# A new order for all steps of a fused linear-attention and gated feed-forward kernel, with other engines and buffers for some of them

## The chip, the core and the metric

The kernel runs on one core of a Trainium2 chip. The metric is the device time of one execution in microseconds (us), inputs and output in HBM. The times and the profiled execution below are of this kernel on such a core.

## The reference, cut to what matters

```python
def _attn_ref(q, k, v, f_logit):          # (4, 8, 768, 48) each, float32
    f = 1.0 / (1.0 + np.exp(-f_logit))
    for t in range(S):                    # S = 768
        state = f[:, :, t, :, None] * state + np.einsum('bhd,bhe->bhde', k[:, :, t], v[:, :, t])
        y[:, :, t] = np.einsum('bhd,bhde->bhe', q[:, :, t], state)

def _moe_ref(x, w_in, w_out):             # x (3072, 384), w_in (384, 2048), w_out (2048, 384)
    h = x @ w_in
    g = h * np.cos(h)
    return g @ w_out

x = y.transpose(0, 2, 1, 3).reshape(3072, 384)
```

The first part is a gated linear attention over 4 batches, 8 heads and 768 positions; its output, with the heads put side by side, is the input of the second part, two matrix products with a gate between them.

## The kernel before, in words

**Pairs and units.** The attention is done in chunks of 128 positions, two chunks at a time: a *pair* is 256 positions of one batch, so there are 12 pairs, three to a batch, numbered 0 to 11. The second part is done in 12 *units* of 256 rows, and unit m needs the output of pair m.

**Steps.** `describe` makes a graph of some 900 named steps; a step is a few instructions on one engine. Of pair n:

- `f`, `k`, `q`, `v`: loads from HBM. Pairs 0 and 1 load f, k and q in halves of four heads (`f0.0`, `f0.1`) and v in halves too; the others load whole tensors. All but `f0.0` stand in the queue of SyncE (SP).
- `ex`, `ln`, and for pairs from 4 on `fx`, `fy`: ScalarE's exponentials and logarithms of the gate; `ad`, `qa`, `ka`: GpSimd's preparations of the gate, q and k; `cum`: cumulative sums by matmul on TensorE; `eb`, `ei`: exponentials of them.
- `qm`, `km`: q and k scaled by those, into one tile `qk`; `tq`, `tk`, `qkt`: `qk` transposed. For pairs 0 to 3 `tq` and `tk` are matmuls and `qkt` copies the result out of PSUM; from pair 4 on `tq` is a transposing DMA in SP's queue.
- `sc`: scores on TensorE; `am`: scores times a mask, by VectorE; `vb`, `vt`: v cast to bf16 and spread (in pairs 0 and 1 `vb` is a scaling of v on line 520, two halves, and `vs` spreads it on TensorE); `ps`, `sj`, `st`, `sz`: the state; `y`, `yi`: the pair's output; `xe`: its copy from PSUM to `x`.

Of unit m: `h` (eight steps of six matmuls, line 728), `co` (cosine on ScalarE, line 733), `g` (the product on VectorE, line 710, which frees the two PSUM banks of `h`), `o` (sixteen steps of four matmuls, line 744; the first number of an `o`, `ot` or `out` is a block of 128 rows, 24 in all), `ot` (PSUM to SBUF), `out` (store). `w0.i` and `w1.i` load a quarter of w_in and w_out as float32 into a buffer of `g`, and `wc0.i`, `wc1.i` cast it to bf16 (line 197); an `h` or `o` needs the quarter that it uses. `zf` is a matmul of zeros that nobody reads, `zsp`, `zqk`, `zvt` clear parts of buffers, and `cqp`, `cqi`, `cqs` make masks and selectors on VectorE.

**What sets the order.** Nothing is scheduled at run time or by a heuristic: the string `ORDER` lists every step once, with its engine (T TensorE, S ScalarE, V VectorE, G GpSimd, Y SP) and, for what the step is first to write, the slot of the buffer (or the PSUM bank) that it goes to. `emit` walks the list and issues the steps in that order. Each engine works through its own instructions strictly in that order and waits, at each, for the semaphores of what it reads and of who used the buffer before. So a step that waits holds up all that stands behind it on its engine, SP's queue included.

```python
    for word in ORDER.split():
        name, how = word.split(":")
        plan.append((G.steps[name], LETTER[how[0]], [int(x) for x in how[1:].split(",") if x]))
```

`SLOTS` gives the number of buffers of each kind (three of v, four of f and so on), and is not changed.

Of the kernel before, what the change touches and what calls it, by code (L numbers as in the profile page):

```python
# [15 lines left out]
B, H, S, D = 4, 8, 768, 48  # L16
# [29 lines left out]
ei2:S ex3:S ex1.1:S k1.0:Y vs0:T4 vt0.0:V2 sz0.00:V cum1.0:T6 ln1.1:S eb1.0:S2 tk0.1:T7 qm0.1:V
qm0.0:G v1.1:Y tk0.0:T0 q1.1:Y w0.1:Y3 ei1.0:S sj0.1:T sz0.11:V2 zqk.2:G w0.0:Y4 tq0.1:T qkt0.1:V2
vt0.1:S qm1.0:G2 zf19:T2 zf20:T2 zf21:T2 tq0.0:T sz0.10:V sc0.1:T2 zf22:T7 cum1.1:T1 ln3:S2
qkt0.0:V4 yi0:T0 am0.1:V0 sc0.0:T6 w0.2:Y1 am0.0:V1 eb1.1:S zf23:T5 tq1.0:T4 vb1.1:V0 cum3:T2
ei1.1:S km1.0:G tk1.0:T eb3:S0 w0.3:Y0 qm1.1:G sj1.0:T6 y0:T7 vb1.0:V ei3:S xe0.1:V0 km1.1:G xe0.0:V  # L50
zf24:T5 zf25:T5 ps1.0:T1 zf26:T5 ps1.1:T sz1.01:V0 vs1:T2 qkt1.0:S0 tq1.1:T0 vt1.1:S2 wc0.1:G
sz1.00:V tk1.1:T wc0.0:G sj1.1:T vt1.0:V qkt1.1:V4 h0.11:T4 sc1.0:T2 sc1.1:T6 k3:Y1 h0.10:T
sz1.10:V3 sz1.11:V k2:Y0 h0.01:T0 zsp.1:V am1.0:V2 co0.1:S0 h0.00:T co0.0:S1 yi1:T2,3 am1.1:V0
wc0.2:G y1:T xe1.1:S2 h0.20:T6 g0.1:V3 xe1.0:S zvt.1:V wc0.3:G km3.1:G1 h0.21:T co0.2:S0 h1.11:T2
h1.10:T g0.0:V g0.2:V h1.01:T0 q2:Y2 w1.2:Y4 h1.00:T km2.1:G2 h1.20:T4 q3:Y1 h1.21:T co1.1:S3
km2.0:G g1.1:V0 co1.0:S2 g1.0:V h0.31:T2 w1.0:Y1 co1.2:S3 h1.30:T6 tk2.0:T1 qm2.1:G wc1.2:S tq2.1:T0
h0.30:T co0.3:S0 g1.2:V qm2.0:G tk2.1:T km3.0:G qm3.0:G tq2.0:T qkt2.1:V1 tk3.0:T5 qkt2.0:S4 h1.31:T
tk3.1:T4 o0.2:T0 tq3.0:T qm3.1:V tq3.1:T w1.1:Y2 g0.3:V qkt3.0:S0 o3.2:T1 o1.2:T2 o2.2:T3 co1.3:S2
qkt3.1:S3 g1.3:V w1.3:Y4 wc1.0:G o1.0:T o2.0:T sc3.1:T4 wc1.3:G v3:Y1 f4:Y1 v2:Y0 sc2.0:T6 am2.0:V2
wc1.1:S o3.0:T am3.1:V0 o0.1:T o3.1:T o3.3:T ot3:V2 vb3:G2 ex4:S vt3.0:S2 vt3.3:G f5:Y0 sc3.0:T4  # L60
am3.0:V1 ln4:S0 q4:Y0 sc2.1:T6 am2.1:V3 vt3.1:G vt3.2:G vb2:G0 fx4:S ad4:G2 o2.1:T o2.3:T o0.0:T
ps3.0:T4,1 ps3.1:T k4:Y0 ps2.1:T5 ot2:V1 fy4:S ps2.0:T sz3.01:V0 vt2.0:S1 o0.3:T sz3.00:V o1.3:T
q5:Y2 vt2.3:G ex5:S vt2.1:G cum4:T7 y3:T3,4 ln5:S1 v4:Y1 yi3:T fx5:S st2.00:V st2.01:V sz2.01:V1
# [12 lines left out]
km6.0:G2 zvt.0:V yi5:T4,5 vb6:G1 y5:T zsp.0:G co4.0:S2 g4.0:V3 h3.00:T q7:Y0 xe5.1:S0 ka7:G
ps6.0:T5,6 fy6:S km6.1:G ps6.1:T sz6.00:V1 f9:Y0 qa6:G h4.20:T2 qm6.0:G sz6.01:V xe5.0:V h4.21:T
fy7:S co3.0:S2 vt6.0:S2 g3.0:V h4.31:T4 h4.30:T co4.2:S1 co4.3:S0 h5.11:T0 qm6.1:G tq6.0:Y2 f8:Y2
st6.10:V st6.11:V out5:Y h5.10:T g4.2:V qa7:G o6.0:T h4.10:T2 sz6.11:V2 g4.3:V h4.11:T vb8:S0
co5.1:S1 km7.0:G1 qm7.0:G g5.1:V0 ot6:S2 vt6.3:G sz6.10:V h5.21:T4 co4.1:S2 tq6.1:Y4 g4.1:V h5.20:T  # L80
o7.2:T7 vb7:G2 k8:Y1 co5.2:S1 tq7.0:Y0 g5.2:V qm7.1:G km7.1:G ex8:S ex9:S ln9:S0 fy9:S ad9:G2 fx9:S
o7.3:T o7.0:T o7.1:T ot7:V3 tq7.1:Y1 vt7.0:G0 ln8:S1 ps7.0:T0,6 ps7.1:T vt8.0:G1 st7.00:V vt7.2:G
sc6.1:T4 vt6.1:S k9:Y0 sc6.0:T2 fx8:S o9.3:T1 o9.0:T o8.3:T7 am6.1:V1 o8.0:T st7.01:V out7:Y vt7.1:S
sc7.1:T4 am6.0:V3 f10:Y1 sc7.0:T2 o9.1:T q9:Y1 am7.1:V2 o9.2:T ot9:V3 sz7.01:V0 v11:Y2 out9:Y
cum9:T4 eb9:S0 o8.2:T am7.0:V0 ad8:G0 cum8:T1 sz7.00:V o8.1:T ei9:S0 vt6.2:G ka9:G vt7.3:G q8:Y0
km9.0:G1 y6:T4,5 yi6:T f11:Y3 k10:Y2 qa9:G qm9.1:G yi7:T2,3 qm9.0:G xe6.1:V1 fy8:S st7.10:V st7.11:V
sz7.11:V1 ctl:S km9.1:G y7:T sz7.10:V xe7.1:V2 eb8:S2 vt8.1:G ot8:V3 ei8:S2 ka8:G h5.01:T0 xe6.0:S
# [779 lines left out]
```

## Time and profile before

| | us |
|---|---|
| median of 3 runs | 181.04 |
| lowest and highest | 180.32, 181.69 |
| the profiled execution, its own time | 181.73 |
| span of the profiled execution | 179.9 |
| TensorE (PE) busy | 170.9 |
| VectorE (DVE) busy | 132.5 |
| ScalarE (ACT) busy | 132.2 |
| GpSimd (POOL) busy | 97.5 |

The span goes from the first to the last instruction that the profiler saw; 1.8 us of the execution's time lie outside it. A matmul counts as busy from its start to its end, and consecutive ones overlap, so short waits between them don't show as idle time. DMA queue q1 is that of SP; the profile names a load by its tile (`g<-in_moe_w_in_dram` is a quarter of w_in on its way to its buffer).

### The profile page before, as it was taken

How to read it: one execution, taken by the hardware profiler on the slowest of the kernel's cores; microseconds unless marked ns; L12 is line 12 of the kernel's file. 1: busy time of each engine (PE TensorE's matmuls, PEld its weight loads, DVE VectorE, ACT ScalarE, POOL GpSimd, SP SyncE). 2: the span in 40 equal slices, each digit the busy share in tenths (PEclk: the TensorE clock that was granted, in tenths of full speed). 3: DMA queues.
4: the chain of work that ended last, by engine and by line, in shares of the span. 5: the costliest groups of instructions: out<-in, count | busy, mean ns of one | idle time of the engine just before them, and what ended most of it. 6: DMA issues, size and time to landing. Idle time of an engine off the chain costs nothing.

```text
span 179.9 us, 5963 instructions
## 1 busy us (share of the span) xinstructions
PE 170.9 (95%) x2543; PEld 124.4 (69%) x2545; DVE 132.5 (74%) x210; ACT 132.2 (73%) x181; POOL 97.5 (54%) x119
## 2 busy tenths in 40 slices
PE   7989789999999999999969999999999999999992
PEld 2566568965688866787637886678688666877751
DVE  6379997857896999899948798966766884558330
ACT  3698658978799999999959899967685804544232
POOL 4007667964899979869587995595078000000000
PEclk9999999999999999999999999999999999999998
DMA  4999998999999999998989999973003901500023
GB/s 126 306 300 267 333 353 206 348 374 272 247 264 242 195 239 205 284 212 190 242 213 275 271 264 203 224 231 58 4 0 56 206 4 46 175 5 0 0 91 131
DMA packets 70330, 34.46 MB, mean 192 GB/s; under 512 B 59296, under 2 KB 68768, under 8 KB 70304
## 3 DMA queue, kind: packets, MB, share of 16 engines
q1 hardware_dynamic: 69744, 33.69, 78.4%
q8 instruction: 20, 0.33, 0.8%
q10 hardware_dynamic: 560, 0.39, 0.8%
q14 instruction: 6, 0.05, 0.1%
HBM read 25.17 MB, written 4.72 MB: 166 GB/s over the span
## 4 chain that ended last, share of the span: by engine, by line
PE 74%; DMA 14%; SPq 3%; POOL 3%; DVE 2%; ACT 1%; issue 1%; DVEq 0%; POOLq 0%
PE ps L744 32%; PE ps L728 30%; PE ps L680 5%; DMA q<-in_q_dram 4%; DMA g<-in_moe_w_in_dram 4%; SPq L336 3%; PE ps L595 3%; DMA v<-in_v_dram 3%; DMA qkt<-qk 3%; PE ps L626 2%; DVE g L710 1%; POOL qk L507 1%; POOL w_in_bf L197 1%; PE ps L424 1%; POOL qk L503 1%; DVE vq L520 1%
## 5 line engine op out<-in xcount | busy, mean ns | idle before, releaser
L710 DVE TENSOR_TENSOR g<-ps,co 128x1024 bf16<-128x1024 f32 x48 | 58.0, 1221 | 22.6 <-ACT co L733 20.0
L744 PE MATMUL ps<-w_out_bf,g 128*128 128x384 bf16 x384 | 68.4, 326 | 0.0
L728 PE MATMUL ps<-x,w_in_bf 128*128 128x256 bf16 x576 | 67.4, 273 | 0.6 <-POOL w_in_bf L197 0.4
L733 ACT ACTIVATE co<-ps,halfpi 128x1024 bf16<-128x1024 f32 x48 | 52.7, 1115 | 19.1 <-PE ps L728 18.5
L728 PEld LDWEIGHTS <-w_in_bf 128*128 128x128 bf16 x576 | 55.5, 98 | 9.5 <-POOL w_in_bf L197 1.0
L744 PEld LDWEIGHTS <-g 128*128 128x128 bf16 x384 | 35.9, 98 | 21.7
L599 DVE TENSOR_TENSOR am<-ps,pmask 128x1024 bf16<-128x1024 f32 x24 | 28.6, 1217 | 3.9 <-PE ps L595 3.6
L507 POOL TENSOR_TENSOR qk<-k,bi 128x384 bf16<-128x384 f32 x16 | 15.8, 1000 | 7.6 <-issue 7.0
L507 POOL TENSOR_TENSOR qk<-q,b 128x384 bf16<-128x384 f32 x16 | 15.8, 1002 | 0.5
L197 ACT COPY ot<-ps 128x384 f32<-128x384 f32 (+1 forms) x12 | 4.9, 422 | 12.7 <-PE ps L744 12.7
L372 ACT ACTIVATE f<-f 128x768 f32<-128x768 f32 (+1 forms) x14 | 10.4, 751 | 4.4 <-DMA f<-in_f_logit_dram 4.3
L197 POOL COPY vt<-vb 64x384 bf16<-64x384 bf16 x25 | 12.5, 503 | 1.2
L410 POOL TENSOR_TENSOR sp<-ls 128x384 bf16<-128x384 f32 x8 | 8.0, 1000 | 7.3 <-ACT ls L378 6.4
L647 DVE TENSOR_TENSOR ps<-ps,sz 128x192 f32<-128x192 f32 x26 | 9.4, 361 | 0.9 <-PE ps L626 0.5
L197 DVE CAST x<-ps 128x384 bf16<-128x384 f32 x12 | 6.5, 552 | 4.5 <-PE ps L680 4.5
L197 DVE COPY ot<-ps 128x384 f32<-128x384 f32 x14 | 7.7, 554 | 2.8 <-PE ps L744 2.6
L302 PE MATMUL ps<-zero 128*128 128x512 bf16 x25 | 8.5, 464 | 1.4 <-DVE zero L203 1.2
L595 PE MATMUL ps<-qkt 48*64 48x128 bf16 x384 | 8.3, 220 | 1.5 <-DMA qkt<-qk 1.4
L492 POOL TENSOR_TENSOR qk<-q,bq 128x384 bf16<-128x384 f32 x3 | 3.0, 1008 | 11.6 <-DMA q<-in_q_dram 11.4
L386 POOL TENSOR_TENSOR q<-f,q 128x384 f32<-128x384 f32 x8 | 8.0, 1001 | 2.2 <-DMA q<-in_q_dram 2.1
L652 DVE TENSOR_TENSOR sz<-ps,b 128x192 bf16<-128x192 f32 x26 | 8.4, 350 | 0.8 <-PE ps L626 0.6
L786 ACT ACT_TABLE_LOAD x6 | 7.7, 1283 | 1.6 <-PEq L851 1.5
(105 smaller groups left out, 200.8 us busy)
## 6 DMA issues: line engine op xcount, KB each, us to landing
out_dram<-ot SPq DMA_DIRECT2D x22, 192.0 KB, 4.1
f<-in_f_logit_dram SPq DMA_DIRECT2D x10, 384.0 KB, 5.9
k<-in_k_dram SPq DMA_DIRECT2D x10, 384.0 KB, 6.4
q<-in_q_dram SPq DMA_DIRECT2D x10, 384.0 KB, 6.0
v<-in_v_dram SPq DMA_DIRECT2D x10, 384.0 KB, 6.6
g<-in_moe_w_in_dram SPq DMA_DIRECT2D x4, 768.0 KB, 9.6
g<-in_moe_w_out_dram SPq DMA_DIRECT2D x4, 768.0 KB, 8.1
v<-in_v_dram SPq DMA_DIRECT2D x4, 192.0 KB, 4.9
```

Source lines behind the costliest of these rows:

```text
L197: (nc.scalar.copy if e == "ACT" else eng(e).tensor_copy)(out=o, in_=i)
L302: G.step(f"zf{i}", ("PE",), lambda e, dump=dump: nc.tensor.matmul(dump.ap, lhsT=zero[:, 0:128], rhs=zero, start=True, stop=True), writes=[ ...
L372: nc.scalar.activation(out=flat(t.ap), in_=flat(t.ap), func=AF.Exp, scale=-1.0)
L507: G.step(f"{nm}{n}.{u}", ("POOL", "DVE") if cut else ("POOL",), lambda e, u=u, j=j, src=src, dec=dec: eng(e).tensor_mul(out=qkp[u][j].ap[: ...
L595: nc.tensor.matmul(o[64 * h:64 * h + 64, r, 2 * a + g, :].rearrange("p (e n) -> p e n", e=2), lhsT=qkv(u)[s, 1, a, g, h, :], rhs=qkv(u)[s, ...
L599: G.step(f"am{n}.{u}", ("DVE",), lambda e, u=u, sc=sc: nc.vector.tensor_mul(out=am[u].ap.rearrange("p r b n -> p (r b) n"), in0=sc.ap.rear ...
L647: G.step(f"st{n}.{g}{r}", ("DVE",), lambda e, r=r, view=view, S0=S0: nc.vector.tensor_add(out=view(), in0=view(), in1=S0.ap[:, :, r, :]), ...
L680: nc.tensor.matmul(py[g].ap[32 * c:32 * c + 32, C * m:C * m + C], start=(py[g].first and (g, c) not in begun), stop=(py[g].final and left[ ...
L710: nc.vector.tensor_mul(out=o.rearrange("p b (n e) -> p b n e", e=2), in0=ph.ap.rearrange("p (b e n) -> p b n e", e=2, n=64), in1=co.ap.rea ...
L728: nc.tensor.matmul(ph.ap[:, i * T:(i + 1) * T].rearrange("p (g t) -> p g t", t=C), lhsT=w_in_bf[:, kk, f0:f0 + 128], rhs=xa[:, :, kk, :], ...
L733: G.step(f"co{m}.{j}", ("ACT",), lambda e, ph=ph, co=co: nc.scalar.activation(out=co.ap, in_=ph.ap, func=AF.Sin, bias=halfpi), reads=[ph], ...
L744: nc.tensor.matmul(po.ap[:, 0:DM], lhsT=gT.ap[:, j, i * C:(i + 1) * C], rhs=w_out_bf[:, j, :], start=(po.first and j == 4 * s), stop=(po.f ...
```

## The change

`ORDER` is replaced whole: all steps stand in another order, 54 of them on another engine, many in another slot or bank, and the number of `zf` steps goes from 27 to 33. The rest of the program is the same. Of the diff, the beginning of the table and the number:

```diff
-ZEROS = 27
+ZEROS = 33
...
-f0.0:S1 f0.1:Y cqp:V zsp.2:V zqk.1:G cqs:V zvt.2:G ex0.0:S cqi:V ex0.1:S ln0.0:S2 f2:Y3 v0.0:Y1
...
+cqi:V zvt.2:G cqp:V zvt.1:V f0.0:S1 ex0.0:S f0.1:Y ex0.1:S zsp.0:G ln0.0:S0 v0.0:Y2 v0.1:Y vb0.0:V0
```

Counted by engine: ScalarE has 169 steps (173 before), VectorE has 191 (186 before), GpSimd 109 (111), SP 104 (103). Of the casts of v, `vb2`, `vb5`, `vb7` and `vb11` go from GpSimd to ScalarE, and single `vt` steps change places between these two. Seven more `xe` and two more `qkt` go to VectorE. The program switches ScalarE's function table 12 times, as before.

**First place: the start, SP and VectorE.** SP's queue from its first load on, before (the number behind a name is its buffer, so `f_3_102` is slot 3 of f; `128x2x192` is a half of pair 0 or 1, `128x8x96` a whole tensor):

```order
L336 DMA f_1_100<-in_f_logit_dram 128x2x192
L336 DMA f_3_102<-in_f_logit_dram 128x8x96
L336 DMA v_1_110<-in_v_dram 128x2x192 x2
L336 DMA k_1_104<-in_k_dram 128x2x192
L336 DMA f_0_99<-in_f_logit_dram 128x2x192
L336 DMA k_1_104<-in_k_dram 128x2x192
L336 DMA f_2_101<-in_f_logit_dram 128x8x96
L336 DMA q_1_107<-in_q_dram 128x2x192 x2
L336 DMA f_0_99<-in_f_logit_dram 128x2x192
L336 DMA v_1_110<-in_v_dram 128x2x192
L336 DMA k_2_105<-in_k_dram 128x2x192
L336 DMA q_0_106<-in_q_dram 128x2x192
```

The same queue now:

```order
L336 DMA f_1_100<-in_f_logit_dram 128x2x192
L336 DMA v_2_111<-in_v_dram 128x2x192 x2
L336 DMA k_1_104<-in_k_dram 128x2x192
L336 DMA f_3_102<-in_f_logit_dram 128x2x192
L336 DMA f_2_101<-in_f_logit_dram 128x8x96
L336 DMA k_1_104<-in_k_dram 128x2x192
L336 DMA q_2_108<-in_q_dram 128x2x192 x2
L336 DMA v_2_111<-in_v_dram 128x2x192
L336 DMA f_3_102<-in_f_logit_dram 128x2x192
L336 DMA f_0_99<-in_f_logit_dram 128x8x96
L336 DMA k_0_103<-in_k_dram 128x2x192
L336 DMA v_2_111<-in_v_dram 128x2x192
```

Both halves of v of pair 0 (`v0.0`, `v0.1`) moved ahead of the whole f of pair 2, and the first half of v of pair 1 (`v1.0`) ahead of `f1.1` and of the whole f of pair 3. In both orders v of pair 1 goes to the buffer that held v of pair 0, so `v1.0` waits until VectorE has cast pair 0's. That part of VectorE's work before, behind the masks of `cqp` (line 520 is the cast, `x2` its two halves):

```order
L267 MEMSET sp_2_114 128x16x8
L250 MEMSET qsel_75 128x128
L254 COPY qsel_75<-ident_65 64x2x32 x4
L242 TENSOR_REDUCE odd_76<-ident_65 128x2
L243 TENSOR_TENSOR qincl_73<-incl_67,odd_76 128x2x64
L244 TENSOR_TENSOR qstrict_74<-strict_68,odd_76 128x2x64
L245 TENSOR_TENSOR qhalf_77<-half_70,odd_76 128x8
L520 TENSOR_SCALAR vq_0_129<-v_1_110,odd_76 128x4x4x48 x2
L492 TENSOR_TENSOR qk_1_124<-k_1_104,f_1_100 128x2x4x48 x2
```

And now, behind `cqi` and `cqp`:

```order
L267 MEMSET vt_1_135 128x16x2x8
L520 TENSOR_SCALAR vq_0_129<-v_2_111,odd_76 128x4x4x48
L250 MEMSET qsel_75 128x128
L254 COPY qsel_75<-ident_65 64x2x32 x4
L267 MEMSET qk_0_123 128x32x8
L267 MEMSET qk_2_125 128x32x8
L267 MEMSET sp_2_114 128x16x8
L520 TENSOR_SCALAR vq_0_129<-v_2_111,odd_76 128x4x4x48
L492 TENSOR_TENSOR qk_0_123<-k_1_104,f_1_100 128x2x4x48 x2
```

The two halves of the cast stood side by side and behind all the masks; now `cqs` (lines 250 and 254) and three clearings stand between them.

**Second place: GpSimd at the weights.** Before, from the first weight cast on (`g_3_157` holds `w0.1`, then `w0.0`, `w0.2`, `w0.3`; line 503 scales k and q of pairs 2 and 3):

```order
L197 CAST w_in_bf_167<-g_3_157 128x3x512
L197 CAST w_in_bf_167<-g_4_158 128x3x512
L197 CAST w_in_bf_167<-g_1_155 128x3x512
L197 CAST w_in_bf_167<-g_0_154 128x3x512
L503 TENSOR_TENSOR qk_1_124<-k_1_104,f_2_101 128x8x48
L503 TENSOR_TENSOR qk_2_125<-k_0_103,f_3_102 128x8x48 x2
L503 TENSOR_TENSOR qk_2_125<-q_2_108,bq_1_132 128x8x48 x2
```

Now (`w0.0`, `w0.1`, `w0.2`, `w0.3` in turn):

```order
L197 CAST w_in_bf_167<-g_1_155 128x3x512
L503 TENSOR_TENSOR qk_0_123<-k_1_104,f_2_101 128x8x48 x2
L197 CAST w_in_bf_167<-g_0_154 128x3x512
L197 CAST w_in_bf_167<-g_2_156 128x3x512
L503 TENSOR_TENSOR qk_0_123<-q_2_108,bq_2_133 128x8x48
L197 CAST w_in_bf_167<-g_3_157 128x3x512
```

The four quarters stood in one piece; now k and q of pair 2 are scaled between them, and in SP's queue their loads stand there as well: `w0.0`, `k2`, `w0.1`, `q2`, `w0.2`, `w0.3`.

**Third place: SP at the transposes of pairs 6 and 7.** Before (line 558 are the transposes `tq6.0`, `tq6.1`, `tq7.0`, `tq7.1`, line 755 is a store):

```order
L558 DMA_TRANSPOSE qkt_2_139<-qk_2_125 128x8x128
L336 DMA f_2_101<-in_f_logit_dram 128x8x96
L755 DMA out_0_dram<-ot_3_166 128x384
L558 DMA_TRANSPOSE qkt_4_141<-qk_2_125 128x8x128
L336 DMA k_1_104<-in_k_dram 128x8x96
L558 DMA_TRANSPOSE qkt_0_137<-qk_1_124 128x8x128
L558 DMA_TRANSPOSE qkt_1_138<-qk_1_124 128x8x128
```

Now (`tq7.0`, `tq6.1`, `tq7.1`, `tq6.0`, between stores):

```order
L755 DMA out_0_dram<-ot_0_163 128x384
L558 DMA_TRANSPOSE qkt_0_137<-qk_2_125 128x8x128
L558 DMA_TRANSPOSE qkt_2_139<-qk_0_123 128x8x128
L558 DMA_TRANSPOSE qkt_3_140<-qk_2_125 128x8x128
L558 DMA_TRANSPOSE qkt_4_141<-qk_0_123 128x8x128
L755 DMA out_0_dram<-ot_0_163 128x384
```

The loads and the store that stood between the four transposes are gone from there, and both pairs' transposes are mixed. On GpSimd the cast `vb7`, which stood between the scalings of pair 7, is now ScalarE's.

More of the change, by code (lines that the diff above doesn't have):

```diff
@@ L46 @@
[L46 to L63, printed above, removed]
@@ L76 @@
[L76 to L87, printed above, removed]
@@ new lines @@
+tq0.0:T qkt0.0:V1 vt0.0:S zf25:T6 zf26:T4 zf27:T4 sc0.1:T2 am0.1:V2 w0.0:Y1 qm1.0:G zf28:T0 zf29:T0
+sc0.0:T4 ex1.1:S k2:Y1 sj0.1:T ln1.1:S cum1.1:T6 am0.0:V0 ex3:S yi0:T7 sz0.11:V0 eb1.1:S cum2:T2
+w0.1:Y0 sz0.10:V q2:Y2 y0:T5 xe0.1:V0 ln3:S2 ei1.1:S qm1.1:G ei2:S tk1.0:T4 w0.2:Y2 tq1.0:T km1.1:G
+qkt1.0:V1 eb2:S2 w0.3:Y3 cum3:T0 eb3:S1 tq1.1:T7 wc0.0:G km2.0:G0 km2.1:G vb1.1:V0 wc0.1:G zf30:T2
+zf31:T2 tk1.1:T sj1.0:T4 w1.1:Y4 w1.2:Y1 vb1.0:V ei3:S zf32:T2 ps1.0:T6 xe0.0:V qkt1.1:S3 ps1.1:T
+sz1.00:V1 sz1.01:V wc0.2:G sc1.0:T2 v2:Y1 vs1:T0 vt1.0:S1 h0.00:T4 qm2.1:G vt1.1:S am1.0:V1 sj1.1:T
@@ new lines @@
+sz1.10:V2 tk2.0:T7 sc1.1:T2 q3:Y0 am1.1:V3 k3:Y0 h0.01:T co0.0:S3 yi1:T0,1 sz1.11:V qm2.0:V y1:T
+xe1.1:V3 h0.11:T2 tq2.0:T h0.10:T g0.0:V0 xe1.0:S h1.11:T0 qkt2.0:S0 sc2.0:T4 h1.10:T co0.1:S0
+h0.21:T6 am2.0:V2 co1.1:S1 g0.1:V g1.1:V2 wc0.3:G h1.21:T4 h1.20:T co1.2:S0 h1.01:T2 h1.00:T h0.20:T
+g1.2:V h0.30:T0 co1.0:S2 wc1.1:G w1.0:Y3 co0.2:S1 tq2.1:T4 g1.0:V h0.31:T w1.3:Y4 wc1.2:G v3:Y0
+g0.2:V f4:Y2 tk2.1:T co0.3:S2 f5:Y3 o1.1:T5 h1.31:T2 h1.30:T k4:Y2 qm3.0:G2 o2.2:T7 o0.2:T6
+qkt2.1:V1 o1.2:T g0.3:V tq3.0:T0 km3.0:G co1.3:S1 g1.3:V o0.1:T vb2:S0 qm3.1:G v4:Y2 ps2.0:T4
@@ new lines @@
+sz6.00:V co3.0:S2 km7.0:G2 h4.20:T6 h4.21:T co4.2:S3 st6.10:V g3.0:V vt6.0:G g4.2:V h4.30:T0 zsp.1:G
+h4.31:T out2:Y fy6:S qa6:G co4.3:S2 h4.10:T2 qm7.0:G tq7.0:Y0 h4.11:T qm6.1:G co4.1:S1 g4.3:V o6.0:T
+ot6:S1 h5.20:T6 h5.21:T g4.1:V vb7:S0 st6.11:V o8.0:T5 h5.11:T0 co5.2:S0 vt6.3:S km7.1:G qm7.1:G
+h5.10:T o8.2:T tq6.1:Y2 tq7.1:Y3 qm6.0:G sz6.11:V0 co5.1:S1 vt7.2:G1 tq6.0:Y4 o8.1:T vt7.1:G ex9:S
+o8.3:T ln9:S1 g5.2:V4 ex8:S fx9:S vt7.0:S o9.3:T6 sz6.10:V g5.1:V ot8:V0 out8:Y out1:Y o7.3:T7
+ps7.1:T1,0 vt6.2:G ps7.0:T st7.00:V sc6.1:T2 am6.1:V1 sc7.0:T4 ln8:S0 o7.2:T f10:Y0 vt7.3:G am7.0:V0
```

102 lines of the change are left out of this document (57 added, 45 removed).

## The prediction

> **What bounds the kernel now.** I read the page first, then two long windows, then the chain of work that ended last, and only then the waits of single engines.
>
> ```profile
> PE 170.9 (95%) x2543; PEld 124.4 (69%) x2545; DVE 132.5 (74%) x210; ACT 132.2 (73%) x181; POOL 97.5 (54%) x119
> 23.00:93.00 70.00, 67.84 (x1117) 50.76 (x1117) 58.12 (x86) 62.27 (x81) 55.71 (x64) 1.00 1.12 254
> 93.00:176.60 83.60, 83.56 (x1118) 61.55 (x1112) 57.66 (x77) 52.82 (x71) 32.56 (x39) 1.00 0.52 122
> ```
>
> In the windows the columns are the stretch, its length, busy time of PE, weight loads, DVE, ACT and POOL, the granted clock (1.00, full speed), the busy share of the DMA engines and GB/s. From 93 us on PE is idle for 0.04 us of 83.6: no order can take anything visible out of that stage, only add to it. Between 23 and 93 us 2.2 us are idle. What is left is the start, the 23 us before the first big matmuls, in which PE is filled with zeros and small work. The chain, in order of time (start, length, what; left out is PE's own work):
>
> ```profile
> 3.08 5.40 DMA v<-in_v_dram
> ...
> 8.59 1.15 DVE vq L520 x2
> 9.73 0.48 DVE qk L492
> ...
> 14.30 7.20 DMA g<-in_moe_w_in_dram
> ...
> 21.55 1.47 POOL w_in_bf L197
> ...
> 23.07 0.83 PE ps L728 x6
> ...
> 85.34 1.93 POOL qk L507 x2
> ...
> 87.51 4.86 DMA qkt<-qk
> ...
> 168.11 8.46 PE ps L744 x52
> ```
>
> So the chain is: v of pair 0 lands at 3.08 + 5.40 = 8.48, is cast, SP's queue goes on, the first quarter of w_in lands at 21.50, is cast by POOL until 23.02, and at 23.07 PE begins the units. From there it runs to 176.6 with few waits:
>
> ```profile
> PE ps L595 <- DMA qkt<-qk: 1.4, 1, 1.4
> PE ps L575 <- POOL qk L503: 0.4, 1, 0.4
> PE ps L728 <- POOL w_in_bf L197: 0.4, 1, 0.4
> ```
>
> The new order does the same matmuls, save six more of zeros at the start, so its time is the time at which the units begin, plus the same PE work, plus the waits that are left, plus the tail.
>
> **The change part by part.** I add up against the profiled execution's own 181.73 us; the median of the three runs is 0.69 lower, so the sum's difference is put on 181.04 at the end.
>
> *1. The wait for the transposes of pair 7, -1.4.* It stands in the list above (at 92.42 PE waits 1.40 for `tq7.1`). What led to it:
>
> ```profile
> 84.52 0.82 POOL L197 CAST vb<-v 128x768 bf16<-128x768 f32 x1
> 81.86 0.38 SPq L336 DMA_DIRECT2D f<-in_f_logit_dram  x1
> 82.35 0.51 SPq L755 DMA_DIRECT2D out_dram<-ot  x1
> 82.97 1.59 SPq L558 DMA_TRANSPOSE qkt<-qk  x1
> 84.61 0.57 SPq L336 DMA_DIRECT2D k<-in_k_dram  x1
> 85.28 3.49 SPq L558 DMA_TRANSPOSE qkt<-qk  x2
> ```
>
> `vb7` held POOL for 0.82 just ahead of the last two scalings (1.93), and on SP a load of f (0.38), a store (0.51) and a load of k (0.57) stood between the transposes. Now `vb7` is ACT's and the four transposes follow each other: 0.82 earlier on POOL and 1.46 less in the queue. Ahead of the last scores stand four `o` steps, as before. Either amount alone covers half of the wait, both more than all. I take it as gone; the bounds are 0 and -1.4.
>
> *2. The wait of 0.6 at 37 us, -0.6.*
>
> ```profile
> 36.98 0.81 PE L744 MATMUL ps<-w_out_bf,g 128*128 128x384 bf16 x4
> 38.24 0.62 PE L575 MATMUL ps<-ident,qk 128*128 128x128 bf16 x8 [0.44 <-POOL qk L503]
> 81.20 0.65 PE ps L744 x4
> 74.24 0.66 PE ps L728 x6
> ```
>
> Four such matmuls take 0.65 where the next follow at once (third row, of the chain; the fourth is the same for six of line 728), so 38.24 - 36.98 - 0.65 = 0.6 is lost, for `qm3.0`, whose q arrived late. The new order has `tq3.0` further behind: after h0, h1 and four `o`. What is late next is k of pair 3, whose scaling has five more steps of slack. -0.6, bounds 0 and -0.6.
>
> *3. The tail, -0.2.*
>
> ```profile
> L197 ACT COPY ot<-ps 128x192 f32<-128x192 f32 x4 | 1.1, 322 | 3.8 <-PE ps L744 3.8
> 176.59 0.54 ACT ot L197 x2
> ```
>
> The last two copies were both ACT's (0.54); now one is DVE's, so one copy, 0.32, stands before the store. The store itself stays.
>
> *4. k2 and q2 between the quarters of w_in, +0.6.*
>
> ```profile
> 21.55 1.46 POOL L197 CAST w_in_bf<-g 128x1536 bf16<-128x1536 f32 x1 [1.45 <-DMA g<-in_moe_w_in_dram]
> 23.86 1.47 POOL L197 CAST w_in_bf<-g 128x1536 bf16<-128x1536 f32 x1 [0.85 <-DMA g<-in_moe_w_in_dram]
> 25.86 1.47 POOL L197 CAST w_in_bf<-g 128x1536 bf16<-128x1536 f32 x1 [0.52 <-DMA g<-in_moe_w_in_dram]
> ```
>
> POOL casts a quarter as it lands, so 768 KB come every 2.0 to 2.3 us; half of that, 1.1, is my estimate for the 384 KB of k2 or q2. The third quarter then lands 1.1 + 2.2 + 1.1 + 2.2 = 6.6 behind the first and is cast 1.47 later. From the first `h` to `h0.21`, the first user of that quarter, stand six `h` of 0.66 and seven small steps of about 0.3 (two of them, the eight matmuls of line 575, take 0.62 in the rows of 2): 6.0, while the cast is done at 6.6. PE waits 0.6. Bounds: 0, if small steps take longer, and 1.2, if k2 and q2 take half as long again.
>
> *5. The beginning of the units, +0.4.* This is the term with the widest bounds.
>
> ```profile
> 7.34 0.84 ACT L372 ACTIVATE f<-f 128x768 f32<-128x768 f32 x1 [1.39 <-DMA f<-in_f_logit_dram]
> L520 DVE TENSOR_SCALAR vq<-v,odd x4: 615/970/1348, 8.6 to 19.2; 128x768 bf16<-128x768 f32 x4
> 4.19 0.62 DVE L254 COPY qsel<-ident 64x64 bf16<-64x64 bf16 x4
> L267 DVE MEMSET qk<- 128x256 uint32 x1 | 0.3, 272 | 0.0
> 9.76 0.60 SPq L336 DMA_DIRECT2D v<-in_v_dram  x1
> ```
>
> Both halves of v take the place in the queue that f2 had, with the same bytes, and f2 was there at 7.3. So v lands 1.2 earlier. But DVE does one half of the cast (0.62 is the shortest of the second row), then `cqs` (0.17 + 0.62), two clearings of qk (0.27 each), one of sp (0.17) and only then the other half (0.62): 7.3 + 2.8 = 10.1, where the cast was done at 9.73 before. `v1.0` waits for it and goes out at 10.1 instead of 9.76. With it five more loads stood ahead of the first quarter: six issues in 14.30 - 9.76 = 4.54, 0.6 to 0.76 each. Now there are eight, so that the quarter is issued 0.3 + 1.3 = 1.6 later at most, 1.0 later if none of them has to wait. The bytes ahead of the quarter are the same, and part of its 7.20 to landing was a queue still full, so I take less than half of the 1.0: +0.4. Bounds: -0.5 if v lands right behind f, since the cast would then be done a good microsecond earlier, and +1.6 if the landing follows the issue.
>
> *6. New waits for engines and PSUM banks, +0.6.*
>
> ```profile
> L733 ACT ACTIVATE co<-ps,halfpi 128x1024 bf16<-128x1024 f32 x48 | 52.7, 1115 | 19.1 <-PE ps L728 18.5 <-DVE g L710 0.3
> L710 DVE TENSOR_TENSOR g<-ps,co 128x1024 bf16<-128x1024 f32 x48 | 58.0, 1221 | 22.6 <-ACT co L733 20.0
> L786 ACT ACT_TABLE_LOAD x6 | 7.7, 1283 | 1.6 <-PEq L851 1.5
> ```
>
> An `h` pair takes PE 1.31, its `co` 1.12, its `g` 1.22; there are four pairs of banks. A row of `h` runs dry if ACT comes late to its first `co`, behind a table load of 1.28. In the new order two such rows (units 2 and 3, units 5 to 7) and the last scores of pair 5, whose mask now stands behind two others on DVE, come out within half a microsecond of the edge; I put 0.2 on each of the three. Bounds: 0, as before, and 2.4, a whole `g` in two places.
>
> The six more zero matmuls stand where PE waits for loads, and cost nothing as long as it does; without that cover they would cost 6 x 0.22.
>
> Sum: -1.4 - 0.6 - 0.2 + 0.6 + 0.4 + 0.6 = -0.6, or 181.1 beside the profiled 181.73 and **180.4** beside the median.
>
> *A rule weighed.* Two rows bear on work that DVE and POOL do at once:
>
> ```profile
> 17.93 2.59 DVE L520 TENSOR_SCALAR vq<-v,odd 128x768 bf16<-128x768 f32 x2
> 18.80 1.31 POOL L492 TENSOR_TENSOR qk<-k,f 128x384 bf16<-128x384 f32 x1
> ```
>
> The cast of v of pair 1 takes twice its 0.62 a half where POOL scales k and q, and POOL's own step takes 1.31 instead of 1.0. The Trainium skill, "SBUF — State Buffer", section "SBUF: two separate sides", says that VectorE and GpSimd share one port pair as an exclusive lock, so that the later of two such instructions stands still until the first is done. The trace agrees in sign and size. By that rule the new place of `qm2.0` on DVE, among POOL's weight casts, speaks against the change: it may stand for up to a cast's 1.47, with `xe1.1` and the first `g` behind it, and the sum would be about 0.5 higher; by the rows alone it costs 0.3.
>
> **The rivals.**
>
> *Faster.* v lands right behind f, the units begin 0.5 earlier, and 6 costs nothing: -1.4 - 0.6 - 0.2 + 0.6 - 0.5 = -2.1, or 178.9. For it: PE idles in the start, and nothing else there is long. Against it: f2 as the second load of SP's queue came only at 7.3, and SP's issue, not the bytes, may set the pace. Chance 0.30.
>
> *Slower.* `v1.0` starves the DMA queue. Everything behind it in SP's queue, the weights among it, waits for the second half of one cast that was moved behind four other DVE steps. The turning point is a landing of v at 9.73 - 2.8 = 6.9, less than the 7.3 taken above: later than that, the move costs more than the earlier load brings. If v lands as late as now, at 8.48, the cast ends at 11.3 and the first quarter is issued 1.5 + 1.3 = 2.8 later than now, of which I count 2.2 as in 5 (the queue is empty by then). With only the gains 1 and 3, with 4, and with 6 between its value and its bound (1.2), the sum is -1.6 + 2.2 + 0.6 + 1.2 = +2.4: 183.4. For it: the chain of waits of before goes through this very cast. Chance 0.22, with other new waits of the same size counted in.
>
> *The change does not do what it says*: the casts of v still meet GpSimd's work, vb1 takes 2.6 again instead of 1.3 and the state of pair 1 is late by 1.3; since the first quarter is cast only at 23, most of that is hidden, and the time is about 180.9, inside the forecast.
>
> **How the numbers follow.** Forecast, within 1% of 181.04 (179.2 to 182.9; about what a measurement of this kernel can tell from no change): 0.48. Faster by more: 0.30; slower by more: 0.22. The range leaves out a tenth on each side: below it takes in the faster rival without 4 (0.6), 178.3, rounded to 178.2; above, most of the slower rival, up to 183.0.
>
> **What the profile after would show.** Step 5: the second cast half of pair 0 ends near 10.1 and `v1.0` goes out right after it; the first `h` starts between 22.6 and 24. Step 4: `h0.21` is preceded by a wait for POOL's third weight cast. Step 1: no wait of PE for `qkt` by DMA. Step 2: no wait for POOL's line 503. Step 6: PE's idle time from the first `h` on below 1 us, with ACT's `co` waiting for PE rather than the reverse. Wrong would be the prediction if the first `h` moved by more than 1.5, or if PE showed a wait of over a microsecond behind 93 us.

## The result, and the profile after

The changed kernel is slower by 0.8%: median 182.09 us of eleven runs (180.61 to 182.53) beside 180.83 (179.46 to 182.60) for the kernel before, ratio 1.0079, 95% interval 1.0055 to 1.0103. A second set of eleven runs gave 1.0049 (1.0013 to 1.0084). The forecast was 180.4, slightly faster. (Ratios and intervals leave out disturbed runs, those over 1.5% above the kernel's fastest, and medians do not: three of the changed kernel's second eleven are such and lift its median, 181.77, by 0.8, so kernels are compared below by their ratios.)

The two profiled executions that can be laid side by side first took 181.73 (before) and 181.79 (after), 0.06 apart, which is not the difference of the medians. So both kernels were run and profiled once more; these profiles are called the second ones (before 180.50, after 180.95).

The list of PE's waits, of the changed kernel's first profile and then of its second (what waited, for what; total, count, longest):

```profile
PE ps L569 <- POOL qk L492: 2.2, 4, 0.7
PE ps L626 <- issue: 1.2, 1, 1.2
...
PE ps L728 <- DVE sz L652: 0.2, 1, 0.2
```

```profile
PE ps L569 <- POOL qk L492: 1.2, 2, 0.7
PE ps L728 <- POOL w_in_bf L197: 0.5, 1, 0.5
...
PE ps L595 <- DVE ot L197: 0.4, 1, 0.4
```

The wait for the transposes (line 595 for `qkt` by DMA, 1.4 before) and the one for POOL's line 503 are gone. New is line 569, the transposes of pair 1, which wait for POOL's scalings: that lies ahead of the first `h`. The waits of line 728 in both lists stand at the first `h` itself. The 1.2 us of line 626 (at 77 us, released by nothing shown) is missing from the second profile; it was one execution's. The kernel before, second profile, from its first `h` on:

```profile
PE ps L595 <- DMA qkt<-qk: 1.5, 2, 1.2
PE ps L744 <- POOL w_out_bf L197: 0.3, 1, 0.3
PE ps L626 <- POOL vb L197: 0.2, 1, 0.2
```

Here the wait at 90 us stands again (1.2 of the 1.5); the 0.6 at 37 us does not. The windows of the second profiles, before and then changed, from the first `h` to 93 us:

```profile
21.50:93.00 71.50, 69.27 (x1125) 51.79 (x1125) 59.71 (x86) 62.77 (x81) 55.84 (x65) 1.00 1.12 255
```

```profile
24.30:93.00 68.70, 68.64 (x1110) 51.26 (x1110) 58.38 (x85) 59.98 (x78) 54.30 (x64) 1.00 1.05 261
```

PE idles 2.2 us of 71.5 before and 0.06 of 68.7 after. So in the middle the new order gains 2.2 us between these two, and the loss is in the beginning. There, the chain of the changed kernel's first profile is (start, length, what):

```profile
2.42 4.15 DMA v<-in_v_dram
...
6.68 0.62 DVE vq L520
7.30 0.15 DVE qsel L250
...
8.20 0.27 DVE qk L267
...
8.47 0.27 DVE qk L267
8.74 0.14 DVE sp L267
...
8.90 0.62 DVE vq L520
9.52 0.48 DVE qk L492
10.00 0.15 SPq L336
```

It reads like the edit: v, half the cast, `cqs`, the clearings, the other half, and behind it SP's queue. SP's rows show what stood still (q0.1 and q0.0; v1.0; f1.1 and f3; the first quarter of w_in):

```profile
6.10 1.28 SPq L336 DMA_DIRECT2D q<-in_q_dram  x2
9.55 0.60 SPq L336 DMA_DIRECT2D v<-in_v_dram  x1
10.19 1.27 SPq L336 DMA_DIRECT2D f<-in_f_logit_dram  x2
...
15.48 0.60 SPq L320 DMA_DIRECT2D g<-in_moe_w_in_dram  x1
```

From 7.38 to 9.55 SP issues nothing. Between 10 and 11 us the DMA engines then had little to do (the windows of the changed kernel, and under them those of before; the last two columns are the DMA engines' share and GB/s):

```profile
10.00:11.00 1.00, 0.96 (x14) 0.85 (x15) 0.14 (x1) 0.88 (x3) 0.00 (x0) 1.00 0.28 78
```

```profile
10.00:11.00 1.00, 1.00 (x32) 0.85 (x29) 0.75 (x2) 1.00 (x4) 0.00 (x0) 1.00 1.11 309
```

What waited for those bytes is POOL. Its rows behind 20 us, changed kernel, first profile:

```profile
20.92 1.39 POOL L492 TENSOR_TENSOR qk<-k,f 128x384 bf16<-128x384 f32 x1
22.25 1.80 POOL L197 CAST w_in_bf<-g 128x1536 bf16<-128x1536 f32 x1
```

The first quarter had landed at 21.98, but POOL scaled k of pair 1 until 22.3, and its cast then took 1.80. In the second profile POOL was done with the scalings at 21.96 and idled 0.83 us until the quarter had landed:

```profile
22.79 1.46 POOL L197 CAST w_in_bf<-g 128x1536 bf16<-128x1536 f32 x1 [0.83 <-DMA k<-in_k_dram]
```

The row names a load of k, but that landed only at 24.03; the quarter, issued at 16.04, took 6.7 us and landed at 22.7. So in one execution POOL's own work held up the cast, in the other the landing. The first `h` in the changed kernel's first and second profile, and in before's second one:

```profile
24.32 0.82 PE L728 MATMUL ps<-x,w_in_bf 128*128 128x256 bf16 x6 [0.15 <-DVE sz L652]
24.31 0.83 PE L728 MATMUL ps<-x,w_in_bf 128*128 128x256 bf16 x6 [0.48 <-POOL w_in_bf L197]
21.51 0.83 PE L728 MATMUL ps<-x,w_in_bf 128*128 128x256 bf16 x6
```

The `sz` of the first row comes, in the chain, behind the same scalings of POOL. In before's first profile the first `h` started at 23.07. POOL's rows in before's second profile:

```profile
18.74 1.31 POOL L492 TENSOR_TENSOR qk<-k,f 128x384 bf16<-128x384 f32 x1
19.99 2.87 POOL L197 CAST w_in_bf<-g 128x1536 bf16<-128x1536 f32 x2
```

There POOL casts the first two quarters with no idle time ahead. In the profile that the prediction used it had idled 1.45 us for the quarter, which took 7.20 us to land after its issue at 14.30. In this one it was issued at 12.79 and landed at 19.07, 6.28 later.

### The profile page after: what moved, and what is told of

It is laid out like the page before. It is cut to its first block, busy times and chain, and to the rows that moved or that the text cites. A ratio compares the mean times of both kernels' runs of the same rounds, so it can differ in the third digit from the quotient of the medians.

```text
span 180.0 us, 5972 instructions
## 1 busy us (share of the span) xinstructions
PE 171.4 (95%) x2549; PEld 125.0 (69%) x2551; DVE 134.0 (74%) x215; ACT 131.6 (73%) x178; POOL 94.9 (53%) x117
## 4 chain that ended last, share of the span: by engine, by line
PE 82%; DMA 5%; SPq 3%; DVE 3%; issue 2%; ACT 1%; POOL 1%; POOLq 0%; DVEq 0%
PE ps L744 35%; PE ps L728 33%; PE ps L680 5%; PE ps L595 3%; DMA q<-in_q_dram 3%; SPq L336 3%; DMA v<-in_v_dram 2%; PE ps L626 2%; POOL qk L492 1%; PE ps L575 1%; PE ps L424 1%; DVE vq L520 1%; DVE g L710 1%; ACT co L733 1%; PE ps L431 0%
## 5 line engine op out<-in xcount | busy, mean ns | idle before, releaser
L744 PE MATMUL ps<-w_out_bf,g 128*128 128x384 bf16 x384 | 69.4, 326 | 0.0
L728 PE MATMUL ps<-x,w_in_bf 128*128 128x256 bf16 x576 | 68.6, 273 | 0.2 <-DVE sz L652 0.2
L197 POOL COPY vt<-vb 64x384 bf16<-64x384 bf16 x27 | 13.5, 502 | 3.0 <-PE ps L680 1.8
L197 ACT COPY ot<-ps 128x384 f32<-128x384 f32 (+1 forms) x15 | 6.5, 446 | 11.0 <-PE ps L744 11.0
L197 DVE CAST x<-ps 128x384 bf16<-128x384 f32 x19 | 10.1, 551 | 3.7 <-PE ps L680 3.7
L396 POOL TENSOR_TENSOR k<-k,f 128x384 f32<-128x384 f32 x8 | 8.0, 1002 | 7.4 <-ACT ot L197 2.7
L302 PE MATMUL ps<-zero 128*128 128x512 bf16 x31 | 9.4, 439 | 1.2 <-DVE zero L203 1.2
L197 DVE COPY ot<-ps 128x384 f32<-128x384 f32 (+1 forms) x11 | 5.9, 534 | 5.5 <-PE ps L744 3.0
L595 PE MATMUL ps<-qkt 48*64 48x128 bf16 x384 | 9.1, 220 | 0.0
L595 PEld LDWEIGHTS <-qkt 48*64 48x64 bf16 x384 | 6.5, 106 | 2.9 <-issue 2.1
```

The lines of the kernel that those rows point to most:

```text
L197: (nc.scalar.copy if e == "ACT" else eng(e).tensor_copy)(out=o, in_=i)
L302: G.step(f"zf{i}", ("PE",), lambda e, dump=dump: nc.tensor.matmul(dump.ap, lhsT=zero[:, 0:128], rhs=zero, start=True, stop=True), writes=[ ...
L595: nc.tensor.matmul(o[64 * h:64 * h + 64, r, 2 * a + g, :].rearrange("p (e n) -> p e n", e=2), lhsT=qkv(u)[s, 1, a, g, h, :], rhs=qkv(u)[s, ...
L728: nc.tensor.matmul(ph.ap[:, i * T:(i + 1) * T].rearrange("p (g t) -> p g t", t=C), lhsT=w_in_bf[:, kk, f0:f0 + 128], rhs=xa[:, :, kk, :], ...
L744: nc.tensor.matmul(po.ap[:, 0:DM], lhsT=gT.ap[:, j, i * C:(i + 1) * C], rhs=w_out_bf[:, j, :], start=(po.first and j == 4 * s), stop=(po.f ...
```

## The experiments

The table gives each kernel's median, its ratio to the kernel before with the 95% interval, and from its profile the start of the first `h` and the rest of the span behind it. One step of PE, `sc1.0` (0.4 us), stands behind the first `h` in the old order and ahead of it in the new one, and `sj1.1` (0.2) the other way round.

| kernel | median | ratio | first `h` | rest of the span |
|---|---|---|---|---|
| before, first / second profile | 180.83 / 180.5 (one run) | 1 | 23.07 / 21.51 | 156.8 / 157.2 |
| changed, first / second | 182.09 / 181.77 | 1.0079 / 1.0049 | 24.32 / 24.31 | 155.7 / 154.9 |
| a_slot | 179.65 | 0.9978 (0.9955 to 1.0001) | 22.99 | 154.5 |
| a_cast | 179.70 | 0.9977 (0.9948 to 1.0005) | 23.32 | 154.7 |
| a_loads | 179.91 | 0.9988 (0.9964 to 1.0012) | 22.84 | 155.5 |
| a_best | 179.33 | 0.9959 (0.9927 to 0.9991) | 21.99 | 154.7 |
| b_t90 | 180.57 | 1.0017 (0.9984 to 1.0051) | 21.89 | 156.4 |
| b_t90o | 181.22 | 1.0054 (1.0016 to 1.0092) | 21.88 | 158.5 |
| b_t90s | 179.67 | 1.0007 (0.9971 to 1.0043) | 22.06 | 155.6 |
| b_v | 180.90 | 1.0051 (1.0015 to 1.0086) | 23.50 | 155.6 |
| b_late | 181.27 | 1.0064 (1.0034 to 1.0095) | 23.01 | 156.5 |

Beside each set of runs the kernel before had a median of 180.06 to 180.23, 180.83 in the first.

**Both kernels again.**

> The kernel before, unchanged, for a second profile of it. The profiled execution that the prediction was made from took 181.73 us where the median of eleven is 180.83, so the two waits that I counted as gains (1.4 us ahead of sc7.1 at 90 us, 0.6 us ahead of tq3.0 at 37 us) may belong to that one execution. Theory 'the gains were not there to be had': the second profile has neither the 1.4 us at 90 us nor another wait of over 0.5 us in its place, and its own time is 180.8 or less. Rival 'the gains are real': the wait at 90 us is there again with 1.2 to 1.6 us, and the 0.6 us at 37 us too. Either way the first big matmul should start at 23.0 us, within 0.3.

> The changed kernel, unchanged, for a second profile and more times. Its one wait of over half a microsecond behind the first big matmul is 1.42 us between ps6.0 and h4.20 at 77 us, released by nothing that the profile shows. Theory 'a wait of the new order': it is there again, with 1.2 to 1.6 us. Rival 'a single disturbance': it is gone and the own time is below 181. The first big matmul should start again at 24.3 us (within 0.3), since the start is set by transfers. Median against the kernel before: 0.6 to 1.3 us more.

Neither theory on before holds whole: the wait at 90 us is real (1.2 to 1.4), that at 37 us is not, and others of 0.2 to 0.3 stand elsewhere. My "23.0 in either case" was wrong: 21.51. The four later profiles with before's beginning untouched or nearly so (b_t90, b_t90o, b_t90s and this one) lie at 21.5 to 22.1, so the 23.07 of the prediction's profile was the late one. The changed kernel's 24.3 repeats.

**Where is the beginning lost? a_slot** (buffer 0 of v instead of buffer 2):

```
-... ei0.0:S ln1.0:S2 v1.0:Y2 ex2:S ...
+... ei0.0:S ln1.0:S2 v1.0:Y0 ex2:S ...
```

> The changed kernel with one digit changed: v1 is loaded into buffer 0 of v, not into buffer 2, where v0 lies, so that v1.0 need not wait in SP's queue for the cast vb0.1. Order of everything as in the changed kernel. Theory 'SP stops at v1.0': v1.0 is issued at 7.4 us instead of 9.55, the transfers behind it run on without the gap at 10 to 11.5 us, k and q of pair 1 land 1.5 to 2 us earlier, the first big matmul starts at 22.5 to 23.3 instead of 24.3, and the time falls by 1.0 to 1.5 us against the changed kernel, to about 181.0 or lower. Rival 'the load of f of pair 3 and the other loads put ahead of k and q of pair 1': the bytes ahead of them are the same, the queue was only briefly empty, so they land at most 0.5 us earlier and the time changes by less than 0.3 us.

One digit is worth 1.3 us by the ratios (1.0049 to 0.9978, run side by side; the medians, 181.77 and 179.65, lie 2.1 apart), and the intervals of the two ratios do not meet. SP's rows of it:

```profile
6.09 1.28 SPq L336 DMA_DIRECT2D q<-in_q_dram  x2
7.42 0.61 SPq L336 DMA_DIRECT2D v<-in_v_dram  x1
8.07 1.26 SPq L336 DMA_DIRECT2D f<-in_f_logit_dram  x2
...
13.18 0.61 SPq L320 DMA_DIRECT2D g<-in_moe_w_in_dram  x1
```

From 7 to 13 us it moved 300 GB/s, the changed kernel 228 (second profile):

```profile
7.00:13.00 6.00, 5.63 (x95) 3.61 (x93) 5.14 (x16) 4.73 (x10) 1.01 (x1) 1.00 1.11 300
```

```profile
7.00:13.00 6.00, 5.55 (x94) 3.54 (x93) 5.11 (x16) 4.74 (x10) 1.01 (x1) 1.00 0.81 228
```

72 GB/s over 6 us are 0.43 MB, 1.4 us at 300 GB/s; the first `h` starts 1.32 earlier. Order, engines and bytes are the same in both, so the wait of `v1.0` is shown as the cause of this part. The two profiled executions differ by 1.65 (180.95 to 179.30): 1.32 in the beginning, the rest mainly the wait of line 595 for `ot` at 111 us, which a_slot lacks. It is a part of the beginning's loss and not the whole: the 22.99 of a_slot is still 0.9 to 1.5 later than the first `h` of the old order in its other profiles (21.5 to 22.1).

**a_cast and a_loads**: the two other ways out of the same wait.

```
-... v0.1:Y vb0.0:V0 k0.1:Y1 cqs:V ... zsp.2:V vb0.1:V cum0.1:T5 ...
+... v0.1:Y vb0.0:V0 vb0.1:V k0.1:Y1 cqs:V ... zsp.2:V cum0.1:T5 ...
```

```
-... ln1.0:S2 v1.0:Y2 ex2:S ... eb0.0:S f1.1:Y f3:Y0 qm0.1:V ...
+... ln1.0:S2 ex2:S ... eb0.0:S f1.1:Y f3:Y0 v1.0:Y2 qm0.1:V ...
```

> The changed kernel with one step moved: on DVE the second half of the cast of v of pair 0 (vb0.1) stands right behind the first half again, ahead of cqs and the clearings of qk and sp. Buffers and SP's queue as in the changed kernel. Theory 'the cast that was moved behind four DVE steps holds SP's queue': vb0.1 ends near 8.3 us instead of 9.9, v1.0 goes out at 8.3, the first big matmul starts 1.0 to 1.5 us earlier than the 24.3 of the changed kernel, and the time is 1.0 to 1.8 us below it, a little above that of the kernel with the other buffer (179.65). Rival 'buffer 0 for v1 helps in another way (a later load that waited for buffer 2)': the time stays within 0.4 us of the changed kernel's 181.8.

> The changed kernel with one step moved: v1.0 stands behind the second half of f of pair 1 and f of pair 3 in SP's queue, so that these two go out while the cast vb0.1 is awaited. v1.0 itself is issued no earlier than before, 9.5 to 9.9 us. Theory 'the empty DMA queue is what costs, not the lateness of v': of the 2.2 to 2.5 us that SP stands still, 1.3 are now filled with two issues, so the first big matmul starts about half of a_slot's gain earlier (23.5 to 24.0 instead of 24.3) and the time is 0.7 to 1.3 us below the changed kernel's. Rival 'v of pair 1 came too late for pair 1's own state': v1 lands as late as in the changed kernel, so the time is within 0.3 us of it.

a_cast gets the same back (0.9977) by the cast's place alone, so the step that was moved is named. Its first `h` gains only 1.0 in this profile, because the beginning ends there in another wait:

```profile
PE ps L616 <- DVE vq L520: 1.4, 1, 1.4
```

a_loads gets 1.1 us back by its ratio, as its theory has it, and its first `h` starts at 22.84, earlier than I expected, though `v1.0` is issued at 9.46 as in the changed kernel. So v of pair 1 was not needed earlier; what cost was that loads which wait for nothing stood behind one that waits.

**a_best**: a_slot, and v of pair 1 behind k and q of pair 1.

```
-... v1.0:Y2 ... k1.0:Y0 cum1.0:T5 v1.1:Y eb1.0:S0 ... am0.1:V2 w0.0:Y1 ...
+... k1.0:Y0 cum1.0:T5 eb1.0:S0 ... am0.1:V2 v1.1:Y0 v1.0:Y w0.0:Y1 ...
```

> The changed kernel with v1 in buffer 0, as in a_slot, and with both halves of v1 moved behind k and q of pair 1 in SP's queue, just ahead of the first quarter of w_in: v of pair 1 is cast only at 20 us, and k and q of it are scaled from 15 us on. Theory 'pair 1's k and q set when POOL is free for the weight cast': they land 1.2 us earlier than in a_slot, POOL is done with them 1 us earlier, the first quarter (which lands at 20.6 in a_slot) is cast without a wait behind POOL's own work, the first big matmul starts at 22.2 to 22.7 instead of 23.0, and the time is 0.3 to 0.8 us below a_slot's 179.65. Rival 'the first quarter's own landing sets the beginning': within 0.2 us of a_slot.

It has the best median of all, 179.33, and is the only one whose whole interval lies below 1. POOL is free when the quarter comes, as the theory has it, and now the quarter's landing sets the beginning. POOL's rows, then DVE's for both halves of the cast, which meets next to none of POOL's work:

```profile
18.21 1.00 POOL L492 TENSOR_TENSOR qk<-k,f 128x384 bf16<-128x384 f32 x1
20.47 1.46 POOL L197 CAST w_in_bf<-g 128x1536 bf16<-128x1536 f32 x1 [1.26 <-DMA g<-in_moe_w_in_dram]
```

```profile
19.16 1.14 DVE L520 TENSOR_SCALAR vq<-v,odd 128x768 bf16<-128x768 f32 x2
```

The first `h` starts 1.0 earlier than in a_slot, at 21.99, where most profiles of the old order have it. The 0.3 us between the medians is the theory's lower figure, and less than the two intervals tell apart.

**Is the wait at 90 us worth 1.4? b_t90, b_t90o, b_t90s** (all from the kernel before).

```
-... o7.2:T7 vb7:G2 k8:Y1 co5.2:S1 ... tq7.1:Y1 vt7.0:G0 ...
+... o7.2:T7 vb7:S2 co5.2:S1 ... tq7.1:Y1 k8:Y1 vt7.0:G0 ...
```

> The kernel before with only that part of the change that was to take away the 1.4 us at 90 us: the cast vb7 is ACT's instead of POOL's, and the load of k of pair 8 stands behind tq7.1 in SP's queue. Theory 'the gain is real' (the term of -1.4 us of the prediction): faster than the kernel before by 0.8 to 1.4 us, and the wait of PE for the transposes of pair 7 is gone from the profile. Rival 'most executions of the kernel before do not have this wait, or it is given back in the next row of units': the median is within 0.3 us of the kernel before, even if the wait of sc7.1 is gone.

The transposes are no longer waited for, and the time stays: the rival held. The list of PE's waits, then DVE's, from 80 us on:

```profile
PE ps L424 <- DVE ot L197: 1.5, 1, 1.5
```

```profile
DVE ot L197 <- DMA out_dram<-ot: 2.2, 1, 2.2
```

`ot9` waits for its buffer until the store `out7` has landed, and `cum8` waits for `ot9`'s PSUM bank. b_t90o is b_t90 with `out7` ahead of the loads of k:

```
+... tq7.1:Y1 out7:Y k8:Y1 ...
```

> As b_t90 (vb7 on ACT, the load of k of pair 8 behind the transposes), and the store out7 goes out right behind tq7.1, ahead of the loads of k of pairs 8 and 9. In b_t90 the wait for tq7.1 was gone, but ot9 waited 2.2 us for the buffer that out7 empties, and cum8 behind it waited 1.5. Theory 'given back to the next late thing': with out7 issued 1.3 us earlier this second wait shrinks by 1.2 to 1.5 us too, and the kernel is 0.8 to 1.4 us faster than the kernel before. Rival 'a third wait takes its place' (the masks of the scores on DVE, of 1.22 us each, or the late k8 and k9): within 0.4 us of the kernel before.

```profile
PE ps L728 <- DVE ot L197: 2.1, 1, 2.1
```

The wait moved on once more, to `h6.00` behind `ot8`, which needs the same buffer after `out9`. b_t90s is b_t90 with `ot9` in another buffer:

```
-... out1:Y st4.01:V ... ot9:V3 ... qm8.1:G out2:Y o12.2:T4 ...
+... out1:Y out2:Y st4.01:V ... ot9:V1 ... qm8.1:G o12.2:T4 ...
```

> As b_t90, and ot9 is written into output buffer 1 instead of 3; for that the store out2, which empties buffer 1, goes out behind out1 at 62 us instead of at 98. In the kernel before, buffer 3 alone carries ot7, ot9 and ot8 one after another, each waiting until the store of the one before has landed (92.8 and 97.5 us in b_t90). Theory 'buffer 3 is what is late behind the transposes': neither ot9 nor ot8 waits for a store, PE shows no wait of over 0.5 us between 85 and 101 us, and the kernel is 1.0 to 1.6 us faster than the kernel before. Rival 'the stretch is bound in several places': a wait of about a microsecond shows up at another place there, and the time is within 0.4 us of the kernel before.

Now PE's longest wait between 80 and 101 us is 0.2, and the rest of the span is 155.6, 1.2 to 1.6 below before's. The mechanism is as the theory has it. The time is not shown: the median is 0.54 lower, but the ratio's interval runs from -0.3% to +0.4%.

**b_v and b_late**: single moves in the kernel before.

```
-... ln0.0:S2 f2:Y3 v0.0:Y1 v0.1:Y vb0.1:V0 ...
+... ln0.0:S2 v0.0:Y1 v0.1:Y f2:Y3 vb0.1:V0 ...
```

```
-... zqk.1:G cqs:V zvt.2:G ... vb0.1:V0 k0.0:Y1 vb0.0:V ...
+... zqk.1:G zvt.2:G ... vb0.1:V0 k0.0:Y1 cqs:V vb0.0:V ...
```

> The kernel before with only this: SP's queue reads both halves of v of pair 0 behind the first f, ahead of f of pair 2. All else stays as before, the casts vb0.1 and vb0.0 one behind the other. Theory 'that part of the change helps and only the cast's new place harms': v lands 0.8 to 1.2 us earlier, v1.0 and everything behind it is issued 0.5 to 0.7 us earlier, the first big matmul starts at 20.8 to 21.5 us, and the time is 0 to 0.7 us below the kernel before. Rival 'f of pair 2, a load of twice the bytes per issue, fills the DMA queue better at that place': it starts at 21.5 to 22.3 and the time is the same or up to 0.6 us more.

> The kernel before with one step moved the harmful way: cqs (0.8 us on DVE) stands between the two halves of the cast of v of pair 0, so that v1.0 waits 0.8 us longer. Theory 'each microsecond that SP stands still at v1.0 is a microsecond of the beginning': v1.0 is issued at 9.7 us instead of 8.9, the first big matmul starts 0.5 to 0.9 us later, and the time is 0.4 to 0.9 us more than before. Rival 'the price comes only with f of pair 1 and 3 behind v1.0, as in the changed kernel': here they are ahead of v1.0, the transfers run on meanwhile, and the time is within 0.3 us of before.

b_v is 0.5% slower, for a reason that neither theory had: f of pair 2 lands at 8.60, and ACT, in the old order, wants it ahead of the gates of pair 0:

```profile
ACT f L372 <- DMA f<-in_f_logit_dram: 2.6, 1, 2.6
```

So in the old order ACT loses what the earlier v might bring; in the new one `ex2` stands behind `ei0.0` and `ei0.1`. What the earlier v brings there by itself was not tried. b_late is 1.2 us slower by its ratio for a cast that ends 0.9 later relative to v's landing, with `v1.0` at 10.32. That fits the theory and exceeds its upper figure a little; but `cqs` also delays pair 0's own steps on DVE there, so it supports a_slot and proves nothing alone.

## Why the prediction was wrong

The step that failed is **term 5**, the beginning of the units: +0.4, and it measured +1.25 between the first profiles and +2.8 between the second ones. The second of these is past the 1.5 that the prediction itself named as a sign of being wrong. The first half of the term was right: the second cast half ended at 9.52 and 9.9 (10.1 forecast), and `v1.0` went out behind it. Wrong was what followed from it:

- I took the quarter's landing as the only condition for the first `h`, and put it 0.4 later. In the first profile the quarter was issued at 15.48 (15.3 by the issue count) and landed 0.48 later than in the prediction's profile, but POOL was not free: k of pair 1 landed 1.5 to 4.3 us later (k1.0 at 17.54 instead of 16.04, k1.1 at 19.26 instead of 14.91), and POOL's last scalings began only when q1.1 had landed at 19.84. In the second profile POOL was free, and the quarter, issued at 16.04, landed at 22.7, against 12.79 and 19.07 in before's second profile. The stop of SP's queue moves both conditions, and the later one sets the first `h`.
- I counted the delay of SP's queue in issues and not in bytes: while SP stood for 2.2 us, the DMA engines emptied their queue. v landed at 6.57 and 6.93, ahead of and just at the turning point of 6.9 that I gave for the slower rival, and `v1.0` still cost 1.3 us, because with f1.1 and f3 behind it nothing else could fill the queue. The slower rival had the right mechanism and the wrong point.
- Adding to one execution: the 23.07 from which I counted was 1.0 to 1.6 later than the first `h` of the other executions with that beginning. Taking the sum's difference over to the median put that loss into the kernel before as if it were lasting.

The rest was forecast at -1.0 (terms 1, 2, 3, 4 and 6) and measured -1.1 and -2.3. Of that, 0.3 is only `sc1.0` moved ahead of the first `h`, less `sj1.1` moved behind it. That the first figure comes so near is luck, for a wait of 1.2 that did not repeat stands in it. Beginning and rest together make the profiles differ by 0.1 and 0.5, where the two ratios say 1.4 and 0.9 us; which stage holds what is missing no profile here shows. In parts: **term 1** went as taken, the wait is gone in both profiles; b_t90 shows that this needs more than its two named causes, since in the old order one output buffer takes over. The changed order writes `ot8`, `ot7` and `ot9` into two buffers. **Term 2** was one execution's wait; the kernel before has others in its second profile, 0.8 in all, and the changed one has none ahead of 93 us there. **Term 3** has the wrong sign in both profiles: the last two copies do not run at once, and the last one ends 0.71 us after the first begins, where it was 0.54. The last copies of the changed kernel:

```profile
176.70 0.32 ACT L197 COPY ot<-ps 128x192 f32<-128x192 f32 x1 [1.47 <-PE ps L744]
...
177.05 0.36 DVE L197 COPY ot<-ps 128x192 f32<-128x192 f32 x1 [2.39 <-ACT ot L197]
```

DVE waits for ACT's copy of the other half. **Term 4** (+0.6) did not come: behind the first `h` PE waits for none of POOL's casts in either profile, and the 0.5 of line 728 above is the wait for the first quarter, which belongs to term 5. **Term 6** (+0.6) is 0.4 in the second profile and 1.2 in the first, the wait that did not repeat.

The rival that the casts of v still meet POOL's work held too (DVE, changed kernel, first profile):

```profile
20.84 1.89 DVE L520 TENSOR_SCALAR vq<-v,odd 128x768 bf16<-128x768 f32 x2
```

The two halves take 1.89 where a_best's take 1.14, beside POOL's 1.39 and 1.80 above. What that costs by itself was not tried. On the rule weighed (the Trainium skill, "SBUF — State Buffer", section "SBUF: two separate sides"): `qm2.0` on DVE took 0.55 between two of POOL's casts in both profiles. In the first it began as a cast ended (27.34 and 27.37), in the second it stood for 0.23 until one ended, though it reads nothing of that cast:

```profile
27.79 0.56 DVE L503 TENSOR_TENSOR qk<-q,bq 128x384 bf16<-128x384 f32 x1 [0.23 <-POOL w_in_bf L197]
```

So the trace agrees with the rule in sign, here and at the cast of v, but the 1.47 that it allowed did not come about, nor any wait of PE behind it. The prediction's "and size" says more than its two rows show: both instructions grew there, and their lengths do not tell which one stood.

## What to carry to other kernels

A load that must wait for its buffer stops every load behind it in an in-order queue: before moving the step that frees the buffer, look at what stands behind that load, and give it another buffer or let loads that wait for nothing go first. Take the base of a sum from more than one execution where a transfer ends the wait, and ask which second condition (here POOL's own work) would set the same moment if that transfer came as usual. When a wait is taken out, follow the next user of each buffer down the stage; one output buffer used three times in a row carried the same 1.5 to 2 us to the next place twice.

## What the runs showed of the hardware

The same DVE cast of half a v took 0.62 us with POOL idle and, in a_cast, 1.33 and 1.81 beside POOL's work, which grew less. DVE's two halves there, then POOL's steps at the same time (the weight cast takes 1.46 elsewhere, the two scalings 1.96):

```profile
18.95 3.06 DVE L520 TENSOR_SCALAR vq<-v,odd 128x768 bf16<-128x768 f32 x2
```

```profile
19.94 1.66 POOL L197 CAST w_in_bf<-g 128x1536 bf16<-128x1536 f32 x1
21.57 2.27 POOL L503 TENSOR_TENSOR qk<-k,f 128x384 bf16<-128x384 f32 x2
```

And the landing of one and the same load moves by more than most edits here are worth: the first quarter of w_in took 7.20 us from issue to landing in one execution of before and 4.95 (14.29 to 19.24) in b_t90s, issued at the same moment.
